# Sliding-window attention and a gated feed-forward: the first k and q loads split by head and by token

## The chip, the cores and the metric

The kernel runs on one core of one Trainium2 chip. TensorE (PE in the profile) multiplies matrices, VectorE (DVE), ScalarE (ACT) and GpSimd (POOL) work on SBUF, and SyncE (SP) only issues transfers here. Loads that POOL issues go through one software queue and may change the type on the way (float32 in DRAM to float16 in SBUF); loads and stores that SP issues go through a hardware queue and keep the type. All of them run on the core's 16 DMA engines. The metric is the device time of one execution in microseconds; three runs of the kernel before gave 304.77, 305.67 and 306.55, median 305.67.

## The reference

For 8 batches, 8 heads, 576 tokens and 64 numbers per head, each token attends to itself and the 63 tokens before it; the result, laid out as 4608 tokens by 512, goes through a gated feed-forward.

```python
scores = scale * np.matmul(q, k.transpose(0, 1, 3, 2))
mask = (rel >= 0) & (rel < 64)          # rel = row - column
attn = softmax(np.where(mask, scores, -1e9))
x = (attn @ v).transpose(0, 2, 1, 3).reshape(4608, 512)
gate = np.maximum(x @ w_gate, 0.0)      # 512 x 1536
out = (gate * (x @ w_val)) @ w_out      # 1536 x 512
```

## The kernel before

**Tiling.** The feed-forward runs over nine tiles of 512 tokens. Attention goes by windows of 64 queries against 128 keys. Heads are handled in two halves of four (`hh` 0 and 1), each head on 32 partitions. A load of k or q puts 32 partitions x 1152 numbers per head into `nat`; a DVE transpose of 32 x 32 blocks (`qk_trans`, L254) turns that into `kT` or `qT`, from which TensorE makes scores (`score_run`, L276). ACT takes the exponential, TensorE multiplies by v (`value_block`), DVE divides by the sum (`norm`) and turns the result into `xt` (`turn`, L306), the input of the feed-forward.

**First part (L313).** The start is written out by hand. SP loads k and q of the first four heads of batch 0 as float32 into the room of `vs`, which is not needed yet (L318); DVE and ACT each round one half of every row to float16 (`rounded`, L339). POOL loads k and q of the other four heads (L320), three parts of v, and the four parts of the first column block of w_gate and w_val (L332 to L334). DVE turns k and q of heads 0 to 3, then of heads 4 to 7. Then come scores and exponentials for tokens 0 to 383, values, and the turned `xt`. POOL copies part of v (L378) before it issues anything more.

**Second part (L418).** All later work is a list of named operations (`op`), each with the operations that it comes after. `ORDER` (L24) is a list, written into the kernel, of these operations in the order in which they are issued: each entry has the number of the operation, a letter for its engine (P, A, D, G, S) and the buffers that it takes. A key in microseconds that each `op` carries, and the numbers in `K`, do not reach the chip: an engine simply works through its own entries in the order of the list and waits in each for what it needs. An operation behind a waiting one on the same engine waits too. A PSUM bank passes on when the operation that gives it back is done.

The weights come in column blocks 0, 1 and 2 of 512, each in two halves by input row. Tile 0 uses them plainly: groups of matmuls for gate and value (`direct_halves` L679 for block 0, `direct_block` L636 for blocks 1 and 2), a relu on ACT, a product on DVE, and then w_out in three blocks (L858). Later tiles use a scheme with seven products in place of eight (L784, L948), which needs sums and differences of the weights (`us`, `vs`, L733; `ts`, L892).

The matmul groups of tile 0 are named by their numbers in the changed list (numbers from 11 up are smaller by 6 in the list before): 42 to 63 are block 0, 82, 86, 90 and 94 the gate groups of block 2, 66, 70, 74 and 78 the gate groups of block 1, 98, 102 and 106 (gate) and 99, 103 and 107 (value) the last 128 tokens, 22 the scores of the last three windows of batch 0 in tile 0, 173 and 178 the scores of tile 1, 149 the first group of w_out.

```python
            run = op("scores", key, pe(0.0081 * 8 * n + 0.0268 * n), lambda e: score_run([st[g] for g in range(G)], items),
                     after=after, take=[("bank", st, range(G))])
            exps.append(op("exp", key + kt("e") + 0.6 * g, act(64 * n), exp, after=[run], take=[("p", pp, (g,))], give=[("bank", st, g)]))
```

Of the kernel before, what the change touches and what calls it, by code (L numbers as in the profile page):

```python
# [10 lines left out]
FP32 = mybir.dt.float32  # L11
# [10 lines left out]


ORDER = """  # L24
29S 3G 30S 2G 42P0 36P4 31S 37P5 0G 43P6 1G 32S 33S 38P 11G 44P 34S 48P1 46Ai 54P2 12G 35S 40Aj 56P 39P 58Ak 6G 49P3
51P 7G 55P7 57P 150G 45P 59D 50P 47D 52Al 76P7 4G 41D 80P0 112D 78Am 53D 84P4 148G 114D 16P2615 116D 72P3 20Ag 156G
120D 17Ah 64P5 19A8 5G 82An 60P7 14D 18A9 13D 118D 21P2 24P1 68P0 122G 25D 22D 26D 88P6 70Ao 28D 164G 23D 74Ap 85P1
27D 62Aq 157G 77P0 104D 66Ar 113D 96P7 86As 152G 124D 90At 79D 115G 81P2 98Ak 87D 89P3 83D 8G 93P5 151D 110G 92P4 149D
117G 94Ai 95D 167P6012 160G 121D 73P4 171Aa 119D 154G 123D 65P7 168Ab 9G 106D 61P5 159A 111D 10G 15D 158A 69P2 75D
163G 97P6 91D 169Ac 325G 67D 100P4 170Ad 71D 105G 153D 102Aj 327G 143P3 125D 329G 128P7 99D 161A 107G 162A 177P0 101P1  # L30
178D 108G 155D 180P2 138P4 126G 181D 63D 182D 109G 144P 179D 103D 139P 331G 192D 172P6520 482D 133P1 174Ae 483D 486D
176Af 134P 165D 173A8 485G 145P 175A9 326D 166A 135P 490G 140P 136Al 328D 146Am 183P5 186P0 141As 334G 147S 184D
344P6213 137S 185D 142S 337G 187D 202P4 193D 348Ag 200P5 341G 196D 347Ah 189P3 129P 188D 346Aa 333G 487D 201An 130P
190D 340G 191D 203Ai 195D 215P1 523G 345Ab 214P0 197D 131Ap 224P2 194D 198G 210P 132S 225At 332D 226P3 211Ar 204P6
127G 239P 227Ao 205D 216P 240Ak 212P 199D 217Aq 241P 330D 491G 339S 207P6 213Aj 335S 228P 206A 336S 218D 220P 493G
249P 338S 221Am 208D 233P 343S 242Al 222D 243P6 209G 230P 229As 234D 251P 250Ap 527G 244D 236P 252Ai 354P5 525G 237D
259P 231An 261P 355D 219A 356D 232G 349P0614 245A 357P5 524D 223G 260An 305P7 351Ac 253P2 358D 262As 529G 359D 256P6
352Ad 266P3 263G 254D 246P5 353A8 257D 264P1 255A 709G 268P 489D 271P 265Am 247D 258G 281P4 267Aq 269D 278P5 350A9
274P 248G 282D 276P 275An 279D 360P2 363P0 277As 366P4 532G 369D 284P 235A 286P 364D 531G 361D 310P5 285Ai 362D 270A
367D 238G 377P2 370D 287Ap 306P 365D 280A 373G 294P 371D 378Ao 288P0 368D 296P 283G 289D 311P 297At 372D 295Aj 291P4  # L40
535G 374D 379P3 272D 381P1 375G 380Ar 387P 382D 299P 388Am 389P 298G 300D 391P6 390Aq 393P 292D 301A 384P1 376G 528D
397P 394Aj 307P 536S 398At 273G 395D 342S 312P 290A 385D 537S 383A 302P 534S 410P 308Ak 386G 303D 407P 533S 405P 526D
408Al 392P0 539G 313Ao 315P7 399D 304G 396A 542P1435 411D 406Ar 316P 713G 530D 545Ae 409G 544Af 320P6 546Aa 413P 715G
543Ab 547P2345 538G 414D 412A 321P 710D 549Ag 415G 548Ah 552P1 555P0 550A8 401P3 553D 711G 554D 420P2 551A9 293G 556D
403P4 557D 402An 558P1 561P5 404As 421D 564P0 416P 718G 562D 422A 418P 563D 423P2 400G 417Al 559D 560D 317P 419Ar 568D
433P5 717G 318Am 424D 428P 426P 721G 319S 565D 429Aq 309S 566D 430P1 314S 570D 427Ai 441P2 425G 541S 438P 567D 442Ap
443P0 439Aj 436P 431D 571G 451P 444At 569D 322P 437An 434D 455P4 452As 440G 453P 432A 456D 575P3 454Am 448P 572D 445P
484G 323Aj 449D 463P 576An 324S 465P4 446D 540S 464Ak 435G 461P 712D 720S 458P6 462Ao 577P5 722S 573G 457A 473P 466D
719S 471P 578Ai 468P1 723S 459D 474Aq 585P 469D 460G 476P 586Aj 582P6 477D 467A 479P 725G 587P 492D 472Ap 498P7 583D
447A 475G 579P0 480D 478A 499P 580D 588At 450G 728P4261 716D 500Ap 591P 729Ac 574G 595P 714D 592Aq 589P0 501P4 732Ad  # L50
488G 593D 596Al 502P 730Aa 590P1 481G 503D 603P 731Ab 608P 597D 504S 581A 605P 470G 609D 738P2 606Ar 741P4 601P6 739D
740D 604Am 584G 611P 742D 602As 733P0523 743D 594A 612D 724G 616P 736Ae 494D 599P4 895G 735Af 628P1 899G 621P2 495D
600Ak 618P5 737A8 614P 607G 619D 505P 615Ao 622D 506P 734A9 897G 496D 624P 617Ai 727S 744P3 625An 747P5 598G 750P2
626P 748D 507Ap 749D 631P0 610A 745D 634P 746D 907G 511P 627Am 629D 904G 639P5 497D 630A 508P3 903G 620A 509P 751D
752D 640Ar 623G 636P 632D 643P 635Al 649P 510Aq 644D 613G 646P 650Ak 641P2 754D 515P 642As 633G 647D 656P4 637Aj 753D
# [105 lines left out]
def kernel(  # L161
# [85 lines left out]
    def heads_of(b, name, hh):  # L247
        src = (q if name == "q" else k)[b, G * hh:G * hh + G]
        return src.rearrange("h (i j) d -> (h i) (j d)", i=32)

    def qk_load(b, name, hh):
        nc.gpsimd.dma_start(nat[name, hh], heads_of(b, name, hh))

# [59 lines left out]
    def first_part():  # L313
# [3 lines left out]
        for name in "kq":  # L317
            nc.sync.dma_start(t32[name], heads_of(0, name, 0))  # L318
# [745 lines left out]
```

## Time and profile before

| what | value |
|---|---|
| median of three runs | 305.67 us (304.77 to 306.55) |
| the profiled execution | 306.52 us |
| its span | 304.80 us |
| PE busy | 292.8 us, 96% of the span |
| DVE, POOL, ACT busy | 243.8, 237.5, 213.5 us |
| granted TensorE clock | 0.999 |
| DRAM read, written | 37.75 MB, 9.44 MB |

Loads of the first part by the trace: k and q of heads 0 to 3 issued by SP at 0.82 and 1.26 us, landed at 5.45 and 6.83; k and q of heads 4 to 7 issued by POOL at 1.31 and 2.05, landed at 8.25 and 10.18; three parts of v landed at 11.00, 11.56 and 12.25; block 0 of the weights landed at 13.54, 14.80, 16.04 and 17.87.

| POOL's next loads, in order | issued | landed |
|---|---|---|
| w_gate block 2, second half | 13.61 | 20.00 |
| w_gate block 2, first half | 14.30 | 21.26 |
| w_gate block 1, first half | 15.00 | 22.54 |
| w_gate block 1, second half | 15.69 | 23.79 |
| v of batch 0, 128 rows; 64 rows | 16.39; 17.26 | 24.68; 25.12 |
| w_val block 2, first; second half | 17.93; 18.62 | 26.36; 27.64 |
| q of batch 1, heads 0 to 3 | 20.55 | 29.09 |
| w_val block 1, first half | 21.54 | 30.36 |
| k of batch 1, heads 0 to 3 | 22.82 | 31.75 |
| v of batch 1, 128 rows | 24.08 | 32.92 |
| w_val block 1, second half | 24.97 | 35.15 |
| v of batch 1, 64 rows; 128 rows | 26.83; 27.55 | 35.59; 36.41 |
| k of batch 1, heads 4 to 7 | 28.42 | 37.85 |
| w_out block 0 | 30.52 | 40.37 |
| v of batch 1, 128 rows | 33.53 | 41.21 |
| q of batch 1, heads 4 to 7 | 34.44 | 42.60 |
| w_out blocks 1; 2 | 34.98; 35.71 | 45.21; 47.71 |

How to read the profile: the span is cut into stretches with the busy time of each engine in it; a timeline line has the start, the duration, the engine, the line of the kernel, the operation with output and input, how many were merged, and in brackets the idle time of the engine before it and what ended it. A wait for several things is put under the name of the one that came last by the profile. The load of a transfer is seen from its issue to its landing. DMA records give each packet's start, duration and size.

### The profile page before, as it was taken

Reading aid. Unit: us, or ns where it says so; the run is one execution under the profiler, and the core shown is the slowest. Engines: PE = TensorE matmul, PEld = TensorE weight load, DVE = VectorE, ACT = ScalarE, POOL = GpSimd, SP = SyncE. Lnnn points to the kernel's source line nnn. Section 1 sums busy time; section 2 is a strip of 40 time slices with the busy share of each in tenths; the row PEclk is TensorE's granted clock in tenths of the full one; section 3 lists DMA queues with packets and bytes.
Section 4 is the critical chain, followed back from the end, with each engine's and each line's share of the span. In section 5 each row is a group of like instructions: output and inputs, shape, how many; then the busy total and the mean of one; then the engine's idle time right before and its main releaser. Section 6 shows DMA issues by size and latency. Waiting matters only on the chain.

```text
span 304.8 us, 11222 instructions
## 1 busy us (share of the span) xinstructions
PE 292.8 (96%) x4793; PEld 242.3 (79%) x4793; DVE 243.8 (80%) x424; ACT 213.5 (70%) x417; POOL 237.5 (78%) x235
## 2 busy tenths in 40 slices
PE   7789889999999999999999999999999999999993
PEld 4566655778767888888888888888888888888883
DVE  5966977998878898888888898989788588677772
ACT  4545535888687888778668878777778678778720
POOL 8678986699999799798687798989898376777610
PEclk9999999999999999999999999999999999999999
DMA  7999999988559932962969549261940301100224
GB/s 215 185 184 200 192 202 157 199 179 113 39 86 131 185 72 44 165 61 80 151 69 183 94 65 154 28 163 9 99 107 3 105 5 34 37 1 2 71 94 147
DMA packets 59586, 32.87 MB, mean 108 GB/s; under 512 B 39440, under 2 KB 54416, under 8 KB 59536
## 3 DMA queue, kind: packets, MB, share of 16 engines
q0 software_dynamic: 46672, 18.29, 51.8%
q1 hardware_dynamic: 12720, 13.80, 14.6%
q8 instruction: 37, 0.61, 0.8%
q14 instruction: 13, 0.11, 0.1%
q10 hardware_dynamic: 144, 0.07, 0.1%
HBM read 37.75 MB, written 9.44 MB: 155 GB/s over the span
## 4 chain that ended last, share of the span: by engine, by line
PE 86%; DMA 8%; POOL 2%; DVE 2%; issue 1%; ACT 0%; DVEq 0%; POOLq 0%; ACTq 0%
PE bank L784 49%; PE bank L948 21%; PE bank L858 7%; PE bank L296 4%; DMA wo<-in_moe_w_out_dram 3%; PE bank L290 3%; DMA wg<-in_moe_w_gate_dram 2%; DMA v<-in_v_dram 2%; PE bank L282 2%; PE bank L649 1%; POOL v L261 1%; DVE xw L303 0%; POOL v L378 0%; DVE qT L258 0%; POOL vs L733 0%
## 5 line engine op out<-in xcount | busy, mean ns | idle before, releaser
L818 POOL TENSOR_TENSOR g_sb<-pr,pr 128x512 f16<-128x512 f32 x96 | 121.2, 1277 | 25.5 <-ACT pr L831 6.8
L800 DVE TENSOR_TENSOR pr<-bank,pr 128x512 f32<-128x512 f32 x144 | 94.5, 683 | 28.4 <-PE bank L784 19.1
L793 ACT COPY pr<-bank 128x512 f32<-128x512 f32 x144 | 81.1, 590 | 26.3 <-PE bank L784 21.7
L784 PE MATMUL bank<-xt,vs 128*128 128x256 f16 x384 | 55.7, 273 | 0.0
L784 PE MATMUL bank<-xt,us 128*128 128x256 f16 x384 | 54.9, 273 | 0.0
L809 ACT ACTIVATE pr<-pr 128x512 f32<-128x512 f32 x72 | 45.1, 638 | 2.2 <-DVE pr L800 1.9
L544 ACT ACTIVATE p<-bank 128x512 f16<-128x512 f32 (+1 forms) x68 | 36.7, 594 | 13.8 <-PE bank L290 13.5
L784 PE MATMUL bank<-xt,wg 128*128 128x256 f16 x288 | 42.8, 273 | 0.0
L784 PE MATMUL bank<-xt,wv 128*128 128x256 f16 x288 | 41.8, 273 | 0.0
L784 PEld LDWEIGHTS <-vs 128*128 128x128 f16 x384 | 36.9, 98 | 5.6
L784 PEld LDWEIGHTS <-us 128*128 128x128 f16 x384 | 37.1, 98 | 4.7
L261 POOL DMA_DIRECT2D v<-in_v_dram x40 | 34.9, 878 | 4.0 <-PE bank L296 3.3
L831 ACT ACTIVATE pr<-bank 128x512 f32<-128x512 f32 x48 | 28.1, 604 | 12.2 <-PE bank L784 11.4
L948 PEld LDWEIGHTS <-g_sb 128*128 128x128 f16 x336 | 32.8, 98 | 3.8
L948 PE MATMUL bank<-wo,g_sb 128*128 128x256 f16 x252 | 32.4, 273 | 0.0
L784 PEld LDWEIGHTS <-wg 128*128 128x128 f16 x288 | 27.9, 98 | 4.0
L784 PEld LDWEIGHTS <-wv 128*128 128x128 f16 x288 | 27.9, 98 | 3.3
L948 PEld LDWEIGHTS <-ss 128*128 128x128 f16 x252 | 24.4, 98 | 2.9
L303 DVE TENSOR_TENSOR xw<-bank,r 128x448 f16<-128x448 f32 (+2 forms) x45 | 25.2, 568 | 1.0
L308 DVE STREAM_TRANSPOSE xt<-xw 128x512 f16<-128x512 f16 (+2 forms) x38 | 25.2, 671 | 0.4
L858 PE MATMUL bank<-wo,g_sb 128*128 128x512 f16 x96 | 23.2, 380 | 1.3 <-DMA wo<-in_moe_w_out_dram 1.0
L615 POOL TENSOR_TENSOR xt<-xt 128x512 f16<-128x512 f16 x15 | 17.3, 1156 | 6.5 <-DVE xt L615 4.4
(105 smaller groups left out, 388.5 us busy)
## 6 DMA issues: line engine op xcount, KB each, us to landing
out_dram<-pr SPq DMA_DIRECT2D x35, 256.0 KB, 2.6
k<-in_k_dram POOLq DMA_DIRECT2D x15, 288.0 KB, 6.0
q<-in_q_dram POOLq DMA_DIRECT2D x15, 288.0 KB, 6.5
v<-in_v_dram POOLq DMA_DIRECT2D x32, 128.0 KB, 5.3
v<-v SPq DMA_DIRECT2D x24, 66.0 KB, 2.1
v<-v SPq DMA_DIRECT2D x12, 132.0 KB, 3.0
wg<-in_moe_w_gate_dram POOLq DMA_DIRECT2D x6, 256.0 KB, 7.2
wv<-in_moe_w_val_dram POOLq DMA_DIRECT2D x6, 256.0 KB, 8.9
```

The source lines that it names most:

```text
L261: nc.gpsimd.dma_start(v16s[b % 2][lo:hi, g, :, 0:64], v[b, :, 64 * g - 64 + lo:64 * g - 64 + hi].rearrange("h p d -> p h d"))
L303: nc.vector.tensor_tensor(x, blocks_of(to, n)[:, :, 0:D].rearrange("p s (c e) -> p s e c", e=2), r[:, :, :, None].to_broadcast([128, n, 2, ...
L308: nc.vector.transpose(xt[:, 2 * hh:2 * hh + 2, c0:c0 + n].rearrange("p e (s c) -> p s e c", c=32), x)
L544: nc.scalar.activation(pp[g][:, 0:n].rearrange("p n c -> p (n c)"), st[g][:, 0:64 * n], ACT.Exp, scale=scale)
L784: nc.tensor.matmul(slot[to][:, HT * m:HT * m + HT], w[:, kk, 128 * m:128 * m + 128], x[:, kk], start=(first and m == 0 and kk == 0), stop= ...
L793: lambda e, hold=hold, slot=slot: nc.scalar.copy(hold["x"], slot["A"]),
L800: nc.vector.tensor_tensor(hold["x"], slot[to], hold["x"], ADD)
L809: lambda e: nc.scalar.activation(hold["x"], hold["x"], ACT.Relu), after=[o])
L818: lambda e: VEC[e].tensor_tensor(gh[:, fs:fs + 2, h], pair(a["x"]), pair(b["x"]), MUL),
L831: lambda e, hold=hold, slot=slot, i=i: nc.scalar.activation(hold["x"], slot["A"], ACT.Copy if i else ACT.Relu),
L858: nc.tensor.matmul(bank["b"][:, 0:c1 - c0], gs[t % 2][:, f, 128 * sub:128 * sub + 128], wo[:, f, c0:c1], start=(j == 0 and i == 0), stop=( ...
L948: nc.tensor.matmul(bank[to][:, HD * m:HD * m + HD], a[:, f, 128 * m:128 * m + 128], b[:, f], start=(first and m == 0 and f == 0), stop=(f ...
```

## The change

Only tokens 0 to 383 are scored in the first part, so k and q of tokens 384 to 575 of heads 0 to 3 are not needed there. The changed kernel loads heads 0 to 3 of batch 0 in two steps, and each step in one transfer per head (32 partitions): first 384 tokens of k and of q (eight transfers of 32 x 3072 bytes), later the other 192 tokens (eight of 32 x 1536 bytes) into the room of the second `g_sb` buffer. Both go over SP. The second part is rounded to float16 by ACT or DVE and turned by DVE as operations of the list (`rest_load`, `round`, `rest_turn`: numbers 11 to 16). The scores of the last three windows of batch 0 (22, and 173 for tile 1) now come after these, and the load of batch 1 into the same room after the rest is turned. `QSPLIT` is 0, so its branches are not taken; `FIRST` is not used.

```diff
-        n = S // 32 * D
+        U2 = 2 * U
+        n = U2 // 32 * D
         for name in "kq":
-            nc.sync.dma_start(t32[name], heads_of(0, name, 0))
-        for name in "kq":
-            qk_load(0, name, 1)
+            by_head(nc.sync, t32[name], 0, name, 0, 0, U2)
+        qk_load(0, "k", 1)
...
+            qk_load(0, "q", 1)
...
+    def by_head(queue, to, b, name, hh, lo, n):
+        src = (q if name == "q" else k)[b, G * hh:G * hh + G, lo:lo + n]
+        for g in range(G):
+            queue.dma_start(to[32 * g:32 * g + 32], src[g].rearrange("(i j) d -> i (j d)", i=32))
...
-        qk_trans(0, "k", 0)
+        qk_trans(0, "k", 0, 0, U2)
         rounded("q", nc.scalar.copy, nc.vector.tensor_copy)
-        qk_trans(0, "q", 0)
+        qk_trans(0, "q", 0, 0, U2)
...
+        def load_rest():
+            lo, n = 2 * U, S - 2 * U
+            for i, (name, hh) in enumerate([("k", 0), ("q", 0)] + [("q", 1)] * QSPLIT):
+                to = gs[1].rearrange("p f n -> p (f n)").bitcast(FP32)[:, n // 32 * D * i:n // 32 * D * (i + 1)]
+                load = op("rest_load", kt("l00") + 0.1 * i, {"SP": (1.4, False)}, lambda e, to=to, name=name, hh=hh: by_head(nc.sync, to, 0, name, hh, lo, n),
+                          dma=(0.2, "store", "sp"))
+                rounded = op("round", kt("l00") + 3.0 + 0.1 * i, {"ACT": (0.49, False), "DVE": (0.35, False)},
+                             lambda e, to=to, name=name, hh=hh: (nc.scalar.copy if e == "ACT" else nc.vector.tensor_copy)(nat_of(name, hh, lo, n), to), after=[load])
+                loads[0, name, hh] = rounded
+                turns[0, name, hh] = op("rest_turn", kt("l01") + 0.1 * i, {"DVE": (0.46, False)}, lambda e, name=name, hh=hh: qk_trans(0, name, hh, lo, n),
+                                        after=[rounded])
...
-            after = [turns[b, nm, hh] for b in batches if b for hh in halves for nm in "kq"]
+            after = [turns[b, nm, hh] for b in batches for hh in halves for nm in "kq" if (b, nm, hh) in turns]
```

`ORDER` is another list from its first entries to its last: no engine keeps its old order for more than a few entries, 24 operations sit on another engine, and the number of operations grows by the six new ones. Where the two lists differ at the start, in the numbers of the changed kernel:

| queue | before | changed |
|---|---|---|
| POOL's loads after the first part | as in the table above | w_gate block 2 (second, first half), block 1 first half, v 64 rows, v of batch 1 128 rows, v 128 rows, w_gate block 1 second half, w_val block 2 (first, second half), block 1 second half, q of batch 1, w_val block 1 first half, k of batch 1, v of batch 1 128 rows, q and k of batch 1's heads 4 to 7, v of batch 1 128 rows, w_out 0, 1, 2, v of batch 1 64 and 128 rows |
| TensorE, block 0 | 48 42 43 49 44 50 54 60 62 45 55 57 61 63 51 56 | 48 42 49 43 54 55 60 51 62 50 44 56 57 45 61 63 |
| TensorE, then | 82 86 90, scores 22, 78 70 66 | 82 94 86 90, scores 22, 78 70 66 |
| TensorE, before w_out | ... 173 79 71 67 75 103 106 149 | ... 79 71 173 106 103 107 75 149 |
| TensorE, behind 149 | 134 183 107 186 144 150 | 134 67 183 186 144 150 |
| DVE, first entries | products 65 53 47, weight difference 118, product 59, weight differences 120 122 126 | weight difference 124, products 53 65, rest turn 16, product 47, round 12, rest turn 13, product 59, weight difference 110 |
| ACT, first entries | relu 52 46 64 58 84 | relu 52 58 46 64, round 15, relu 88 92 |

## The prediction

> **What bounds the kernel now.** I read the stretches first, then who TensorE waits for, then its timeline, then the DMA queues. The stretches (PE busy is the second number):
>
> ```profile
> 21.30:40.40 19.10, 17.36 (x288) 12.04 (x288) 16.33 (x37) 10.16 (x21) 16.30 (x20) 1.00 1.47 195
> 40.40:46.00 5.60, 5.27 (x88) 2.93 (x89) 3.42 (x8) 1.26 (x2) 5.08 (x6) 1.00 1.40 202
> 46.00:76.00 30.00, 30.00 (x604) 21.99 (x602) 26.14 (x49) 23.71 (x45) 24.32 (x26) 1.00 1.04 162
> ...
> 286.00:300.00 14.00, 14.00 (x129) 12.33 (x126) 9.40 (x18) 4.74 (x9) 3.82 (x3) 1.00 0.29 95
> ```
>
> From 46 us to its end at 300 us TensorE never pauses and its clock is fully granted. So after 46 us nothing can be gained, only lost, and the change is decided by how late TensorE is when it enters that stretch. Its waits after 14 us:
>
> ```profile
> PE bank L858 <- DMA wo<-in_moe_w_out_dram: 1.0, 1, 1.0
> PE bank L649 <- DMA wg<-in_moe_w_gate_dram: 0.9, 1, 0.9
> PE bank L649 <- DMA wv<-in_moe_w_val_dram: 0.7, 1, 0.7
> ```
>
> and where they stand:
>
> ```profile
> 21.30 2.12 PE L649 MATMUL bank<-xt,wg 128*128 128x384 f16 x12 [0.91 <-DMA wg<-in_moe_w_gate_dram]
> ...
> 35.19 3.34 PE L649 MATMUL bank<-xt,wv 128*128 128x384 f16 x30 [0.70 <-DMA wv<-in_moe_w_val_dram]
> 38.37 1.06 PE L649 MATMUL bank<-xt,wg 128*128 128x128 f16 x16
> 40.42 1.90 PE L858 MATMUL bank<-wo,g_sb 128*128 128x512 f16 x8 [0.99 <-DMA wo<-in_moe_w_out_dram]
> ...
> 45.26 1.02 PE L858 MATMUL bank<-wo,g_sb 128*128 128x512 f16 x4 [0.31 <-DVE xw L303]
> ```
>
> Each is a wait for weights; the 0.31 stands under a DVE name, but block 1 of w_out landed at 45.21. The loads of POOL's queue land one behind another without a gap until 54 us, 1.26 us per 256 KB weight part, 1.42 per k or q, about 0.83 per 128-row v, 0.44 per 64-row v, 2.5 per block of w_out (successive landings). So a transfer's place in that queue is its landing time. The queues on the page:
>
> ```profile
> q0 software_dynamic: 46672, 18.29, 51.8%
> q1 hardware_dynamic: 12720, 13.80, 14.6%
> q8 instruction: 37, 0.61, 0.8%
> ```
>
> The instruction queue matters: its 16 KB packets each hold one DMA engine for 0.9 to 1.1 us (DMA records at 15.8 and 32.4 us), and right behind these two the landings step by 1.8 and 2.1 us (wg, wv: 17.87, 20.00) and by 2.2 us (wv at 35.15) where 1.26 is normal.
>
> **The change, part by part.** The sum is made against the profiled execution (306.52 us, span 304.80, 1.72 around it); the median shown is 305.67, 0.85 lower, and the difference is put on the median.
>
> *First loads.* Two issues of 0.39 and 0.42 us on SP become eight; at 0.42 the last q piece is issued at 0.82 + 7 x 0.42 = 3.8 instead of 1.26. Eight more for the rest stand directly behind them. Their key says 15 us, but nothing on SP holds them except that each waits for the landing of a first piece, so they go at about 4 to 7 us, ahead of v and the weights: no byte leaves the front of the stream. SP's next work is a store at 52.68; nobody is held behind. When does q land (6.83 before)? From below, as a free 66 KB move: 3.8 + 2.1 = 5.9. From above, as the stores at 52.68 to 57.52 that met POOL's loads:
>
> ```profile
> out_dram<-pr SPq DMA_DIRECT2D x35, 256.0 KB, 2.6
> ...
> v<-v SPq DMA_DIRECT2D x24, 66.0 KB, 2.1
> ...
> out_dram<-pr SPq DMA_DIRECT2D x4, 256.0 KB, 5.5
> ```
>
> (the last row is of 52 to 58 us, the first two of the whole run): 3.8 + 5.5 = 9.3. Before, both loads were queued before the first POOL load got a packet (5.09 us); now k of the other four heads, issued at 1.31, can come between, since lone POOL loads show their first packet 1.3 us after issue. The loaded row is nearer: I take 8.
>
> *Rounding and turning for 384 tokens.* By two thirds of their rows the DVE cast of k goes from 0.69 to 0.46 us, each turn from 1.26 to 0.84. That does not pull the front in: q of the other four heads landed at 10.18 and its turn started at 10.20; the v parts landed at 11.0, 11.56 and 12.25. With q at 8: + 0.47 + 0.84 = 9.3, two full turns to 11.8, against 11.46: the first gate matmul (14.44) 0.35 late. Ends: 0 with q at 5.9, 1.6 with q at 9.3.
>
> *Block 0 of gate and value.* 64 matmuls, 5.5 us. The new order puts three groups that need tokens 192 to 383 ahead of those that need the second halves of the weights; those tokens were turned at 16.70, so TensorE stands about 0.8 us there and ends near 20.95 instead of 20.39. This and the late front stay under the wait that ends at 21.30 (0.35 us is left of it), then under the two waits below (0.2 and 0.9 us): a front up to 1.4 us late costs nothing; its upper end would cost 0.2.
>
> *DVE at 21 us.* Its queue now has a weight difference (waits for wg, 21.26; 0.42) ahead of four products of block 0 (0.49 each), the two rest turns (0.42 each) and one rest cast (0.35). These ran at 19.84 to 22.2 before; now they end about 24.9. Waiting for them: a PSUM bank (matmul group 94, 0.3 us late) and scores 22, which now also need the rest turns and the relu behind group 90: start about 25.05 against 23.36 before. TensorE pauses 0.6 us, and then group 78 waits for the second half of wg block 1. That was landing 4 behind 20.00 (23.79); now three v parts stand ahead of it: 22.54 + 0.44 + 0.85 + 0.85 + 1.26 = 25.95, a pause of 0.2 more. From there the steps of the timeline (0.70 for a 384-column group, 1.06 for a 128-column one of block width, scores 0.95) bring TensorE to the first w_out group at about 41.3; nothing between waits more than 0.3 us (scores 173 on the turn of k, landed near 34).
>
> *The w_out load, where it is decided.* Ahead of block 0 of w_out POOL's queue now also has q of batch 1's second half and a 128-row v part, and no longer a 64-row v part: 1.42 + 0.83 - 0.44 = 1.8 us. It landed at 40.37; now 42.2. POOL issues it near 31 (30.52 before), far ahead of the stream, so the order and not the issue counts.
>
> *Are 32-row pieces dearer?* DMA records: 178 ns for 4608 bytes, 96 for 2048, 47 for 1056. Between them 3072 bytes take about 125 and 1536 about 70. Per engine 16 x 178 = 2.85 us become 16 x (125 + 70) = 3.1, and 14 more completion writes of 9 ns add 0.13: +0.4. Ends: -0.3 (POOL's loads fill gaps of SP's) and +0.8 (1536 bytes as dear as 2048, half the gaps unused). I take +0.3: w_out at 42.5.
>
> *Sum.* TensorE starts w_out at 42.5 instead of 40.42: +2.08. Ahead of it is now a 128-column group (107, 1.06) and no longer a 384-column one (67, 0.70): -0.36. Block 1 of w_out follows 2.5 behind block 0 instead of 4.84 (v and q no longer stand between), so the 0.31 at 45.26 goes. +2.08 - 0.36 - 0.31 = +1.4: span 306.2, profiled 307.9, on the median **307.1 us**. What is late next: nothing until the end, if the new order keeps TensorE fed after 46 us as the old one did.
>
> One rule speaks against the pieces more strongly. The 64-row moves of this trace (1056 bytes in 47 ns, 22.5 bytes per ns) show nearly the pace of 128-row loads (25.9), so I price rows by length alone. The Trainium skill, SBUF — State Buffer, "Door 1: The DMA port swizzle", says that a transfer to 32 partitions reaches 8 of 16 ports and gives 189 GB/s against 328 for 128 partitions; by that rule 1.18 MB would take, as an estimate, some 2.6 us longer, and the sum would be near +3.7. The trace's row disagrees so far, on 64 partitions and not on 32.
>
> **Rivals.**
> - *Half-speed pieces, slower.* If a 32-row piece holds its engines twice as long, 2 x 3.1 - 2.85 = 3.3 us at worst and, with POOL's loads filling half, 1.6 at least reach w_out: +2.7 to +4.4, 308.4 to 310.1. It decides from 0.5 us on. This is the case that the page on SBUF describes. For it: pieces of one head lie in one quarter of the partitions. Against: the 47 ns.
> - *New pauses after 46 us, slower.* Every queue's order is new to the end. DVE at 26.14 of 30 us and POOL at 27.25 leave little room; ten pauses like the 0.2 to 0.3 us ones listed for the front, or one late product per tile, give +2 to +4 on top of part of the 1.4: 308 to 311. Against: the old order has no pause there.
> - *w_out on time, not slower.* The slow landing at 35.15 holds 0.95 us that came from an instruction packet hitting the engine already last; of four such packets from 8 to 33 us two did that. If it misses, w_out lands at 41.5, TensorE's own arrival (41.3) nearly decides, and the sum is 41.5 - 40.42 - 0.67 = +0.4: 306.1; with POOL's loads filling SP's gaps, +0.2.
> - *Faster.* If the rest really stood behind the first weights, 393 KB at 25.9 x 16 bytes per ns, 0.95 us, would leave the front, and the 0.91 at 21.30 would go. It would show only if w_out came early too, and its bytes ahead are fixed. At most -1.7: 304.0. The eight rest issues would have to wait, and nothing in the queue makes them.
>
> **How the numbers follow.** Chances: the forecast's case 0.55 (its own range 306.1 to 308.1: one instruction packet less or more is 0.95 either way); half-speed 0.08; new pauses 0.15; w_out on time 0.18; faster 0.04. 0.5% (1.5 us) is about what a measurement of this kernel tells from no change: 304.1 to 307.2 on the median. The forecast's case lies across the upper edge, 0.30 inside and 0.25 above. Faster 0.04, same 0.30 + 0.18 = 0.48, slower 0.25 + 0.08 + 0.15 = 0.48. The range 305.4 to 309.3 leaves out the faster case and the upper half of the two slow ones.
>
> **What would show it.** Right: no wait of TensorE after 46 us; one near 25.5 to 26 for wg; the w_out wait ending near 42.5 and being the last; the SP rest issues at 4 to 7 us; first gate matmul between 14.4 and 16. Wrong: rest issues near 15 us; w_out landing before 41; w_out matmuls starting without a DMA wait; pauses after 46 us; 3072-byte packets far over 125 ns.

## The result and the profile after

The changed kernel takes **308.88 us** (median of six runs, 307.43 to 309.81) against 305.18 for the kernel before (six runs beside it): the ratio is 1.0115, with a 95% interval of 1.009 to 1.014. It is slower by about 3.5 us, where 1.4 was forecast. 308.88 lies inside the range that was given (305.4 to 309.3), but above the forecast's own case (306.1 to 308.1): it is in the part that had been added for two slower rivals.

The traces show less than the medians: the profiled execution after took 308.51 us (span 306.8), that of before 306.52. The trace of before is one of its slower executions (1.3 above the median of the six; later medians of the same kernel are 304.95 to 305.59), that of after one of its faster ones (0.4 below). Of the 3.7 between the medians the pair of traces can explain 2.0; how much of a median a pause in one trace accounts for is therefore read below from medians of edited kernels.

TensorE's timeline of the changed kernel (start, duration, engine, line, operation, number merged, idle time before it and what ended it) answers to the one shown of before. First the start of the one before:

```profile
9.24 0.55 PE L290 MATMUL bank<-qT,kT 32*128 32x64 f16 x48 [1.21 <-DVE qT L258]
10.02 1.56 PE L358 MATMUL bank<-zero 128*128 128x384 f32 x4 [0.23 <-ACT p L370]
...
14.44 0.82 PE L696 MATMUL bank<-xt,wg 128*128 128x192 f16 x8 [0.23 <-DVE xt L308]
```

After:

```profile
11.85 0.55 PE L299 MATMUL bank<-qT,kT 32*128 32x64 f16 x48 [2.73 <-DVE qT L267]
12.64 2.93 PE L374 MATMUL bank<-zero 128*128 128x384 f32 x4 [0.24 <-ACT p L386]
15.50 0.67 PE L299 MATMUL bank<-qT,kT 32*128 32x64 f16 x48
...
18.36 0.82 PE L725 MATMUL bank<-xt,wg 128*128 128x192 f16 x8
...
20.71 0.49 PE L725 MATMUL bank<-xt,wg 128*128 128x192 f16 x4 [0.88 <-DVE xt L317]
...
24.67 2.76 PE L678 MATMUL bank<-xt,wg 128*128 128x384 f16 x16
...
28.01 0.27 PE L291 MATMUL bank<-ident,biasT 32*128 32x128 f16 x5 [0.41 <-ACT pr L688]
...
42.88 1.90 PE L887 MATMUL bank<-wo,g_sb 128*128 128x512 f16 x8 [0.34 <-DVE g_sb L690]
```

The first gate matmul (18.36) starts 3.92 us later than before (14.44), the first block-2 group 3.37 later (24.67 against 21.30), the first w_out group 2.46 later (42.88 against 40.42), and the last matmul ends 2.35 later (302.39 against 300.04). All three weight waits of before are gone: what was waiting is now lateness of TensorE itself, and it begins at 9 us, with a pause of 2.73 for q. The 0.34 at 42.88 has DVE's name, but w_out block 0 landed at 42.83, 0.05 before it; in the kernel before the same step was 0.05 (40.37 and 40.42).

Two lines of DVE's timeline show what the pause waits for, and the table of DMA issues up to 16 us (transfers, KB each, median us from issue to landing) how long a piece took:

```profile
10.43 0.36 DVE L357 CAST q<-vs 128x384 f16<-128x384 f32 x1 [2.52 <-DMA vs<-in_q_dram]
10.96 0.85 DVE L267 STREAM_TRANSPOSE qT<-q 128x384 f32<-128x384 f32 x1 [0.16 <-ACT q L357]
```

```profile
vs<-in_k_dram SPq DMA_DIRECT2D x4, 96.0 KB, 2.9
vs<-in_q_dram SPq DMA_DIRECT2D x4, 96.0 KB, 5.5
...
k<-in_k_dram POOLq DMA_DIRECT2D x1, 288.0 KB, 4.7
q<-in_q_dram POOLq DMA_DIRECT2D x1, 288.0 KB, 6.1
```

Before, the same table had:

```profile
vs<-in_k_dram SPq DMA_DIRECT2D x1, 576.0 KB, 4.6
vs<-in_q_dram SPq DMA_DIRECT2D x1, 576.0 KB, 5.6
```

The last pieces of k and q landed at 6.22 and 10.31 (5.45 and 6.83 before), though they carry a third less; POOL's k and q of heads 4 to 7, which nobody needed yet, landed at 6.04 and 8.14 (8.25 and 10.18). The stretches of the first microseconds (last two numbers: DMA share and GB/s) show it as a flow. Before:

```profile
2.00:3.00 1.00, 1.00 (x44) 1.00 (x41) 0.93 (x4) 0.30 (x2) 0.93 (x5) 1.00 0.76 221
3.00:4.00 1.00, 0.51 (x20) 0.41 (x16) 0.00 (x0) 0.00 (x0) 0.86 (x4) 1.00 0.87 323
4.00:5.00 1.00, 0.61 (x9) 0.27 (x10) 0.18 (x1) 0.00 (x0) 1.00 (x3) 1.00 1.03 424
5.00:6.00 1.00, 1.00 (x5) 0.47 (x4) 0.53 (x1) 0.53 (x1) 1.00 (x2) 1.00 1.11 293
6.00:7.00 1.00, 1.00 (x5) 0.49 (x4) 0.89 (x2) 0.63 (x4) 1.00 (x2) 1.00 1.07 196
```

After:

```profile
2.00:3.00 1.00, 1.00 (x44) 1.00 (x41) 0.93 (x4) 0.31 (x2) 0.93 (x5) 1.00 0.85 177
3.00:4.00 1.00, 0.51 (x19) 0.41 (x16) 0.00 (x0) 0.00 (x0) 0.86 (x4) 1.00 0.61 95
4.00:5.00 1.00, 0.59 (x9) 0.27 (x10) 0.18 (x1) 0.00 (x0) 1.00 (x2) 1.00 1.14 248
```

The three microseconds from 2 to 5 moved 968 KB before and 520 after. Not all of that is lost flow: the records of POOL's loads have the size as written, in float16 (288 KB in the table for 576 KB of float32): 2304 bytes in 192 ns, 12 bytes per ns, where SP's whole loads have 4608 in 178, 25.9. So a stretch full of POOL's packets shows no more than some 196 GB/s (before, 6 to 7 us, share 1.07). The DMA records add whose packets they were: before, POOL's first packet started at 5.09 us, when most of SP's were through; after, it started at 2.77, and in each microsecond from 3 to 7 SP's packets held only 0.16 to 0.26 of the DMA engines' time. POOL's first packets were slow besides: the first twelve took 306 to 909 ns, where the first twelve before took 191 or 192.

The stretches further on (the number before the DMA share is the granted clock):

```profile
14.00:21.30 7.30, 6.12 (x172) 4.23 (x171) 5.84 (x15) 3.37 (x15) 7.24 (x11) 0.87 1.20 196
...
46.00:76.00 30.00, 29.77 (x597) 21.48 (x598) 25.96 (x47) 21.99 (x42) 24.20 (x26) 1.00 1.11 172
```

Behind the pause for q the granted clock fell: 0.87 is the mean of a stretch, and within it the clock was 0.50 from 12.5 to 15.8 us and 1.00 from 15.9 on. Four filler matmuls (products with zeros that nothing reads) took 2.93 us where they took 1.56 before. After 46 us only small pauses (0.23 at 58.6) are new in this execution.

### The profile page after: what moved, and what is told of

The parts are those of the page before. It is cut to its first block, busy times and chain, and to the rows that moved or that the text cites. A ratio compares the mean times of both kernels' runs of the same rounds, so it can differ in the third digit from the quotient of the medians.

```text
span 306.8 us, 11261 instructions
## 1 busy us (share of the span) xinstructions
PE 294.7 (96%) x4793; PEld 243.1 (79%) x4793; DVE 242.5 (79%) x423; ACT 212.9 (69%) x419; POOL 240.4 (78%) x238
## 4 chain that ended last, share of the span: by engine, by line
PE 84%; DMA 7%; POOL 4%; issue 2%; DVE 1%; ACT 0%; POOLq 0%; DVEq 0%; ACTq 0%
PE bank L813 48%; PE bank L977 21%; PE bank L887 7%; PE bank L305 3%; DMA k<-in_k_dram 3%; DMA v<-in_v_dram 3%; PE bank L299 2%; DMA wg<-in_moe_w_gate_dram 2%; PE bank L291 2%; POOL v L270 1%; POOL us L762 1%; POOL q L260 1%; DVE g_sb L690 0%; POOL k L260 0%; POOL v L394 0%
## 5 line engine op out<-in xcount | busy, mean ns | idle before, releaser
L813 PE MATMUL bank<-xt,vs 128*128 128x256 f16 x384 | 56.7, 273 | 0.4 <-issue 0.2
L813 PE MATMUL bank<-xt,us 128*128 128x256 f16 x384 | 55.7, 273 | 0.1
L572 ACT ACTIVATE p<-bank 128x512 f16<-128x512 f32 (+1 forms) x68 | 35.8, 592 | 13.1 <-PE bank L299 13.0
L813 PE MATMUL bank<-xt,wv 128*128 128x256 f16 x288 | 42.8, 273 | 0.0
L813 PE MATMUL bank<-xt,wg 128*128 128x256 f16 x288 | 42.1, 273 | 0.0
L977 PE MATMUL bank<-ts,ss 128*128 128x256 f16 x168 | 21.6, 273 | 0.0
```

The lines of the kernel that those rows point to most:

```text
L572: nc.scalar.activation(pp[g][:, 0:n].rearrange("p n c -> p (n c)"), st[g][:, 0:64 * n], ACT.Exp, scale=scale)
L813: nc.tensor.matmul(slot[to][:, HT * m:HT * m + HT], w[:, kk, 128 * m:128 * m + 128], x[:, kk], start=(first and m == 0 and kk == 0), stop= ...
L977: nc.tensor.matmul(bank[to][:, HD * m:HD * m + HD], a[:, f, 128 * m:128 * m + 128], b[:, f], start=(first and m == 0 and f == 0), stop=(f ...
```

## The experiments

Each was timed against the kernel before on its chip, with the ratio beside it; the time of a kernel alone moves by some tenths with the chip (the kernel before: 304.95 to 305.59).

**Whole first loads.** The new order stays; the pieces and the rest go.

```diff
-        n = U2 // 32 * D
+        n = S // 32 * D
...
-            by_head(nc.sync, t32[name], 0, name, 0, 0, U2)
+            nc.sync.dma_start(t32[name], heads_of(0, name, 0))
...
-    ... lambda e, to=to, name=name, hh=hh: by_head(nc.sync, to, 0, name, hh, lo, n),
+    ... lambda e: None,
...
-    ... lambda e, to=to, name=name, hh=hh: (nc.scalar.copy if e == "ACT" else nc.vector.tensor_copy)(nat_of(name, hh, lo, n), to), after=[load])
+    ... lambda e: None, after=[load])
```

> The changed kernel, but k and q of the first four heads come whole again (576 tokens, one transfer each, rounded whole in the first part); the loads and the rounding of the rest are gone, the turns of the rest and the whole new order of every queue stay. Front theory (the pieces made q land at 10.3 us, the first gate matmul started 3.9 us late, and that lateness is the loss): q lands near 6.9, first gate matmul near 14.6, and the time falls by 2 us or more, to 306 to 307. Queue theory (w_out block 0 stands too far back in POOL's order, 42.8 us): the front comes back all the same, but TensorE then waits for w_out, which lands at 42.2 to 42.6; the time falls by at most 0.6, to 308.2 or more. Two-limits theory (TensorE's own arrival at 42.5 and w_out's landing at 42.8 stand side by side, so that lifting one alone gives little): as the queue theory here; it differs from it in the next kernels.

306.69 us, ratio 1.0041 (1.0013 to 1.0069). Its timeline of TensorE:

```profile
14.95 0.82 PE L725 MATMUL bank<-xt,wg 128*128 128x192 f16 x8 [0.26 <-DVE xt L317]
...
40.08 1.90 PE L887 MATMUL bank<-wo,g_sb 128*128 128x512 f16 x8 [0.90 <-DVE g_sb L690]
...
65.70 0.28 PE L305 MATMUL bank<-v,p 128*32 128x65 f16 x12 [1.15 <-DMA v<-v]
```

q landed at 6.65, the front is back, and 2.2 us of the median with it, as the front theory said. Not expected by any theory: w_out block 0 landed at 40.03 and not at 42.2 to 42.6. The pieces and the rest had pushed the whole stream back, not only q: the first weight part landed at 13.37 here, at 15.11 in the changed kernel, at 13.54 before. And there is a new wait of 1.15 us at 65.7, to which I come below.

**w_out block 0 earlier in POOL's order**, ahead of the v part (166) and the q load (160):

```diff
-... 128D 166G 66P7 130D 72Ao 116D 27P6 160G ... 97D 8G 83P5 ...
+... 128D 66P7 130D 72Ao 116D 27P6 ... 97D 8G 166G 160G 83P5 ...
```

> The changed kernel with one edit in the written order: on POOL's queue the load of w_out block 0 goes ahead of the 128-row v part and of q of batch 1's second half, as before the change. Its landing should move up by 0.83 + 1.42 = 2.2 us, from 42.8 to 40.6. Queue theory: the first w_out matmul starts 1.5 to 2 us earlier and the time falls to about 307. Front theory and two-limits theory: TensorE itself does not get there before 42.5, so the wait of 0.34 goes and no more: 308.3 to 308.9.

309.35 us, ratio 1.0102 (1.0070 to 1.0135): no change. w_out landed at 40.30, and TensorE came to it, without a wait, at 43.24:

```profile
19.23 0.82 PE L725 MATMUL bank<-xt,wg 128*128 128x192 f16 x8
...
43.24 1.89 PE L887 MATMUL bank<-wo,g_sb 128*128 128x512 f16 x8
```

So in the changed kernel the place of w_out does not decide: TensorE itself comes later than the load. The queue theory, which my forecast stood on, falls here.

**Both edits.**

> Both edits together: whole first loads, and w_out block 0 ahead of the v part and the q load. Two-limits theory: only here does the time fall, by about 2 us or more, to 306 to 306.9, with w_out landing near 40.3 and the first w_out matmul at 40.5 to 41.5. Front theory: as with whole loads alone. Queue theory: as with w_out earlier alone. If the new order of the other engines costs something after 46 us, the time stays above 307 though the first w_out matmul is early.

305.34 us, ratio 0.9996 (0.9975 to 1.0017): with whole loads and w_out as early as before, the new order of everything else costs nothing that can be measured.

```profile
14.51 0.82 PE L725 MATMUL bank<-xt,wg 128*128 128x192 f16 x8 [0.23 <-DVE xt L317]
...
39.50 1.89 PE L887 MATMUL bank<-wo,g_sb 128*128 128x512 f16 x8
```

The four kernels as ratios to before:

| | w_out as changed | w_out earlier |
|---|---|---|
| pieces and rest | 1.0115 | 1.0102 |
| whole loads | 1.0041 | 0.9996 |

The pieces and the rest cost 0.7 to 1.1% (2.3 to 3.2 us), whichever way w_out stands. The place of w_out costs 0.45% (1.4 us) with whole loads, where the two intervals just touch, and nothing that can be measured with pieces: the late front hides it. The two-limits theory is right in that part, but wrong in that one edit alone already brought 2.2 us.

**The pieces alone, in the kernel before** (all 576 tokens, four transfers per tensor, no rest, the old order):

```diff
-            nc.sync.dma_start(t32[name], heads_of(0, name, 0))
+            for g in range(G):
+                nc.sync.dma_start(t32[name][32 * g:32 * g + 32], (q if name == "q" else k)[0, g].rearrange("(i j) d -> i (j d)", i=32))
```

> The kernel before the change with one edit: each of the two first loads of SyncE is made in four pieces of one head (32 partitions, 4608 bytes each, all 576 tokens) instead of one transfer; no rest, no new order. q should land late again, 8 to 10.5 us, for eight issues of 0.42 us and POOL's loads between. Front theory: the time rises by 2 us or more, to 307.2 or more. Two-limits theory: the waits of TensorE for weights (0.91, 0.70, 0.99) take up some 2.6 us of a lateness of 3 to 4, so the time rises by 0.3 to 1.3, to 305.5 to 306.5. Queue theory: no more than 0.3. If 32-partition pieces hold the DMA engines longer, w_out lands 1.6 us or more later than 40.4 as well and the time rises by 1.6 or more.

309.95 us, ratio 1.0137 (1.0104 to 1.0170): 4.2 us above before by the ratio, as only the front theory and the clause on dearer pieces allowed.

```profile
20.77 0.83 PE L697 MATMUL bank<-xt,wg 128*128 128x192 f16 x8
...
43.67 1.89 PE L859 MATMUL bank<-wo,g_sb 128*128 128x512 f16 x8
```

The split by head does the damage by itself: q landed at 11.85, the first gate matmul came 6.3 us late, and the waits of 0.91, 0.70 and 0.99 were used up long before w_out. The stream was late as well (first weight part 14.79 against 13.54, w_out 42.19 against 40.37), but TensorE did not come to w_out before 43.67. The other half of the change, 384 tokens in place of 576, helps against this (q at 10.31 in the changed kernel), without making up for it.

**POOL's first loads a little later.**

```diff
+        if not QSPLIT:
+            bands()
         qk_load(0, "k", 1)
...
-        if not QSPLIT:
-            bands()
```

> The changed kernel with one move: GpSimd builds its two masks before it issues the loads of k and q of heads 4 to 7 (now after). Those two issues go from 1.32 and 2.06 us to about 2.7 and 3.4, so their first packets from 2.77 to about 4. If q of the first heads is late because POOL's packets come between the pieces, q lands at 7.5 to 9 instead of 10.3, the first gate matmul starts 1 to 2.5 us earlier than 18.4, and the time falls by 0.7 to 2 us, to 307 to 308.2. If the pieces of 32 rows are slow in themselves, q lands at 9.8 or later and the time does not fall (308.5 to 309.5); it would rise if the two POOL loads, which then land later, come to be what the front waits for.

310.23 us, ratio 1.0170 (1.0136 to 1.0204). A miss: q landed at 10.83, later than in the changed kernel. Its DMA issues say why:

```profile
vs<-in_k_dram SPq DMA_DIRECT2D x4, 96.0 KB, 2.2
vs<-in_q_dram SPq DMA_DIRECT2D x4, 96.0 KB, 6.0
```

POOL's issues (2.27 and 3.01 us) now fell behind the last piece of k and behind the first of q, and its first packet came at 3.72. The pieces of k took 2.2 us (median); those of q, with POOL's packets, 6.0. So pieces of 32 rows are not slow by nature to the extent seen in q.

**q on ScalarE's queue, and then w_out earlier besides.**

```diff
-            by_head(nc.sync, t32[name], 0, name, 0, 0, U2)
+            by_head(nc.scalar if name == "q" else nc.sync, t32[name], 0, name, 0, 0, U2)
```

> The changed kernel, but the four first pieces of q are issued on ScalarE's queue and no longer on SyncE's behind those of k, so that all eight pieces are issued by about 2.2 to 2.6 us (now 4.4). If what makes q late is that its pieces are issued one after another by one engine while POOL's packets start at 2.77, q lands at 6.5 to 8.3 and k a little later than its 6.2; the first gate matmul starts 2 us or more earlier, and the time falls to 306.5 to 307.7. If the shares of the DMA engines decide and not the issue, q still lands at 9 or later and the time stays above 308.

> As the last, with w_out block 0 ahead of the v part and the q load on POOL's queue besides. If the front comes back, this should be worth 1.3 us more, as it was with whole loads (306.69 to 305.34): 305.2 to 306.4. If the front does not come back, it is worth nothing, as in the changed kernel (308.9 to 309.3).

308.08 us (1.0104, 1.0069 to 1.0139) and 308.36 us (1.0095, 1.0061 to 1.0128), neither as low as hoped; the first is above 308, as the expectation has it where the shares of the DMA engines decide. With two engines issuing, k and q share the lateness: in the first k landed at 8.56 (6.22 in the changed kernel), with q behind by little (its cast started at 9.91 without a wait); in the second they landed at 8.46 and 8.63. The first gate matmul came at 17.14, 1.2 earlier, and the first w_out group in the second at 40.96, 1.9 earlier. All of that was lost again in two pauses later on, in the second:

```profile
57.30 0.60 PE L813 MATMUL bank<-xt,vs 128*128 128x256 f16 x4 [0.87 <-issue]
67.79 0.28 PE L305 MATMUL bank<-v,p 128*32 128x65 f16 x12 [1.36 <-DMA v<-v]
```

**More filler in the pause.** Does the lower clock cost time?

```diff
-        keep_hot(st[1][3][:, 0:2 * U])
+        for _ in range(4):
+            keep_hot(st[1][3][:, 0:2 * U])
```

> The changed kernel with three more of the filler matmuls (0.74 us each, multiplied by zeros, nothing reads them) in the stretch in which TensorE waits for q (9.1 to 11.85 us). No data comes earlier. If the loss of clock behind that pause is part of the loss (the four fillers after it took 2.93 us instead of 1.56, the granted clock 0.94 and 0.87), the second run of scores starts 1 to 1.4 us earlier, so does the first gate matmul, and the time falls by 0.5 to 1.4 us, to 307.5 to 308.4. If not, it stays at 308.9.

309.15 us, ratio 1.0136 (1.0102 to 1.0170): no gain, although the front does come earlier. The fillers behind the first scores took 1.56 again and the first gate matmul came 1.1 earlier; the first w_out group was at 41.45, 1.4 earlier; then:

```profile
13.04 1.56 PE L374 MATMUL bank<-zero 128*128 128x384 f32 x4 [0.23 <-ACT p L387]
...
17.26 0.82 PE L726 MATMUL bank<-xt,wg 128*128 128x192 f16 x8
...
56.96 0.61 PE L814 MATMUL bank<-xt,wv 128*128 128x256 f16 x4 [0.46 <-ACT p L573]
67.77 0.28 PE L305 MATMUL bank<-v,p 128*32 128x65 f16 x12 [1.23 <-DMA v<-v]
```

So the lost clock is worth 1.1 us at the front, and pauses further on, the larger near 66 us, took it back. That one is for the moves of v on chip over SP's queue. In this trace the second of them was issued at 61.37 and landed at 67.72, 0.2 behind the q load that POOL issued at 61.86 (67.49). In the changed kernel the first two moves landed in good time (67.04; TensorE came at 67.41).

**All pieces ahead of POOL.** POOL's loads go behind its masks and three sets of constants:

```diff
+        if not QSPLIT:
+            bands()
+        nc.gpsimd.memset(zero32, 0.0)
+        for i in range(2):
+            v_fixed(i, nc.gpsimd)
         qk_load(0, "k", 1)
...
-        for i in range(2):
-            v_fixed(i, nc.vector)
-        nc.vector.memset(zero32, 0.0)
-        if not QSPLIT:
-            bands()
```

> The changed kernel with GpSimd's two loads of heads 4 to 7 held back behind its masks and three sets of constants (which VectorE wrote until now), so that they are issued near 4.5 us and their packets start near 5.8, after the last piece of q has been issued. The four pieces of k of the last kernel but three landed 2.1 to 2.5 us after their issue while no GpSimd packet ran. If GpSimd's packets are what holds the pieces up, all pieces of q now land by 6.5 to 7.3, the wait for q goes, heads 4 to 7 land at 8.5 and 10.7, and the first gate matmul starts at 14.8 to 16; the time falls to 306.7 to 308. If pieces of 32 rows are slow whatever runs beside them, q lands at 9 or later and the time stays at 308.9 or above.

(The kernel that this text counts back to is the one with POOL's first loads a little later.) 308.78 us, ratio 1.0117 (1.0088 to 1.0146): the time does not move. POOL's issues went to 3.70 and 4.44 and not to 4.5. The first piece of q landed at 4.76, 2.1 us after its issue; the other three, in whose time POOL's packets began (5.16), landed at 6.68, 6.92 and 8.71, so that the edit spared one piece and not all. The first gate matmul came at 17.01, 1.35 earlier, but POOL's whole stream had moved back with its first loads (first weight part at 16.08):

```profile
10.25 0.83 PE L299 MATMUL bank<-qT,kT 32*128 32x64 f16 x48 [2.46 <-DVE qT L267]
...
17.01 0.82 PE L725 MATMUL bank<-xt,wg 128*128 128x192 f16 x8
...
42.76 1.90 PE L887 MATMUL bank<-wo,g_sb 128*128 128x512 f16 x8 [0.97 <-DMA wo<-in_moe_w_out_dram]
```

Now TensorE waits 0.97 us for w_out: the front theory's gain met the queue theory's bound, the other side of the table above. The same kernel shows how the pieces flow with nothing beside them (3 to 5 us), and what happens when POOL's packets begin (5 to 6):

```profile
3.00:4.00 1.00, 1.00 (x28) 0.68 (x26) 0.00 (x0) 0.00 (x0) 0.94 (x4) 1.00 0.71 200
4.00:5.00 1.00, 1.00 (x4) 0.45 (x3) 0.36 (x1) 0.49 (x2) 1.00 (x2) 1.00 0.79 219
5.00:6.00 1.00, 1.00 (x5) 0.47 (x4) 0.85 (x1) 0.35 (x3) 1.00 (x3) 1.00 0.87 100
```

200 to 219 GB/s at a DMA share of 0.71 to 0.79, where whole loads reached 323 and 424; and about 100 in the microsecond in which POOL's packets set in. In the kernel before the microsecond of that start moved 293 GB/s, SP's packets among them.

What held the pieces at 200 to 219? SP hands over a piece of 98,304 bytes every 0.46 us, which is 214 GB/s by itself. Two kernels shown above bear on it, from 2 to 3 us: the kernel before with pieces (147,456 bytes each, the same pace of issue), and the first with q on ScalarE's queue (two engines issuing):

```profile
2.00:3.00 1.00, 1.00 (x44) 1.00 (x41) 0.93 (x4) 0.30 (x2) 0.93 (x5) 1.00 0.95 254
2.00:3.00 1.00, 1.00 (x44) 1.00 (x42) 0.93 (x4) 0.31 (x1) 0.93 (x5) 1.00 0.93 283
```

With more bytes per issue, or with a second engine that issues, the pieces flow faster, at a DMA share of 0.93 to 0.95. So it was the pace of issue that held one queue of 96 KB pieces. What would hold them above 283 is not shown, since POOL's packets begin at 2.81 and 3.08 us in these two.

**The q load of the third batch held back**, first with whole loads, then with w_out earlier too. It tests the bound near 66 us.

```diff
-... 348S 531G 257P ... 236P 215G 240D ...
+... 348S 257P ... 236P 215G 531G 240D ...
```

> Whole first loads as before, and in the written order of GpSimd the load of q for the third batch, issued at 60.5 us, goes behind the next product (to about 63.5). With whole loads TensorE waits 1.15 us at 65.7 for the moves of v on SyncE's queue, of which the second took 5.9 us from issue to landing beside that load. If the load holds the moves up, the pause goes and the time falls by 0.6 to 1.1, to 305.6 to 306.1 (that is most of what w_out earlier gave with whole loads, 1.35). If the moves are late for another reason, or another wait takes over, the time stays at 306.4 to 307.

> The three edits together: whole first loads, w_out block 0 earlier, and the q load of the third batch held. If the pause at the moves of v is there in many executions of the kernel with the first two edits (its profiled execution, 304.73, had none; its median is 305.34), the median falls by 0.3 to 0.7, to 304.6 to 305.0. If not, it stays at 305.3.

305.89 us (1.0017, 0.9989 to 1.0046) and 304.85 us (0.9991, 0.9970 to 1.0012). In the first the moves of v landed at 64.1 to 66.0, the q load now being issued at 64.94, and the pause at 65.7 is gone from the trace. Against the kernels without this edit the ratios fall by 0.0024 and 0.0005, in the expected direction; the intervals overlap, so the size is not shown. It also means that part of what the table puts down to the place of w_out may be this pause, which the trace of whole loads has and that of both edits has not. The second is the best kernel of the study, and its interval does not tell it from the kernel before.

**w_out earlier in the kernel before.** Was that wait the bound there?

```diff
-... 86As 152G 124D ... 83D 8G 93P5 ...
+... 86As 8G 152G 124D ... 83D 93P5 ...
```

> The kernel before the change with one edit in the written order of GpSimd: the load of w_out block 0 goes ahead of the load of k of batch 1's second half (1.44 us), so it should land near 38.9 instead of 40.37. In the kernel before, TensorE waits 0.99 us for it at 40.42 and then never again to the end. If that wait sets the end, the time falls by 0.7 to 1.0, to about 0.997 of before (304.3 to 304.7). If the moves of v near 65 us are the next bound right behind it, or a load that now lands 2.5 us later is waited for, the time stays within 0.3 of before.

305.42 us, ratio 1.0005 (0.9987 to 1.0022). No gain: w_out block 0 landed at 38.00 and was not waited for, and block 1, at 44.18, was:

```profile
38.45 1.89 PE L858 MATMUL bank<-wo,g_sb 128*128 128x512 f16 x8
...
44.23 1.89 PE L858 MATMUL bank<-wo,g_sb 128*128 128x512 f16 x8 [1.26 <-DMA wo<-in_moe_w_out_dram]
```

Taking one load forward handed the wait to the next; that the stream as a whole is the bound there would explain it, but is not shown. In its trace the last matmul ended 1.07 earlier than in that of before (298.97), and the medians agree: a difference of 1 us between two single traces is not evidence here.

## Why the prediction was right or wrong

- *Direction and size.* Slower, by 3.5 us and not 1.4. The forecast's case, a late w_out load as the one cause, is not what happened. That 308.88 lies inside the range is luck as far as that case goes: the range reached up there for rivals that had 0.23 together, and the cause was neither of them as I had put it, but a late front.
- *When q lands: the step that failed.* I took 8, with 5.9 and 9.3 as ends; it was 10.31. The upper end came from 256 KB stores met by POOL's loads (5.5 us). The last piece of q took 5.9 from its issue at 4.39, but I had put that issue at 3.8, and I had used the upper row as a bound, though nothing made it one. I had written that POOL's k "can come between" and did not follow it to the end: POOL's packets did not share the engines evenly, they held four fifths of them. The cleanest sign is one piece, the first of q, issued at 2.65 us in three kernels: it landed at 4.76 where POOL's first packet came at 5.16, at 7.94 where it came at 3.72, and at 8.24 (the changed kernel) where it came at 2.77. The Trainium skill, DMA: Bandwidth & Descriptors, "Queues, rings and completion order", says that each engine goes round the queues that have work and drains a whole packet of some 9 to 17 descriptors before it switches. If an engine switched after each transfer, a piece of 32 rows (two records per engine of 134 ns) against a POOL load of 128 rows (eight of 192) would give SP, as an estimate, 0.27 / (0.27 + 1.54) = 0.15 of an engine's time, near the 0.16 to 0.26 of the trace. That condition is mine, and the trace of before does not fit it: POOL's first packet there came at 5.09, when 228 of the 256 packets of SP's two loads had started, and not behind the first load's 128, although the same issue (1.31 us) had its first packet at 2.77 in the changed kernel. No run here changed the number of rows alone, so why POOL's share is so large stays open.
- *The front.* "A front up to 1.4 us late costs nothing" was not tested as such; the front was 3.9 late. The first scores started 2.6 late (11.85 against 9.24), for q. The other 1.3 came behind them, most of it from the clock (1.1 by the filler experiment), which I had left out altogether: four fillers behind the pause took 2.93 in place of 1.56. With whole loads and the new order it was 0.5 late (14.95), and the wait for w_out, 0.90 long, took that up.
- *The wait at 20.7.* I forecast about 0.8 us for tokens 192 to 383, and 0.88 is there, as are 0.87 to 0.88 in the edited kernels with the new order.
- *The waits from 21 to 42 us.* The pause of 0.6 at scores 22 came as one of 0.41, at 28.01 and not near 25. The 0.2 for w_gate at 25.95 did not come: TensorE was late enough (28.45 for group 78, with the load landed at 26.30). The issues of the rest, put at 4 to 7 us, went out at 4.86 to 10.33: the last four waited each for a piece of q.
- *w_out at 42.5: right by two errors.* It landed at 42.83. By their own steps (1.42 and 0.85, less 0.44) the two extra loads are worth the 1.8 that I gave them. But the pieces cost the stream 1.6 us at the first weight part (15.11 against 13.54), not 0.3, and the slow steps of the stream, which I left as they were, gave back some 0.8: 1.83, 2.13 and 2.23 before (2.4 over the normal 1.26) against one of 2.84 after (31.55 to 34.39, 1.6 over). I had put them down to instruction packets. That does not hold for the one after: its packets (20.19, 26.20 and 35.33 us) stand elsewhere, and no slow step follows the first two. What makes such a step is open. With whole loads the same two loads stand ahead of w_out, and it landed at 40.03, no later than before: from trace to trace the slow steps differ by as much as the whole term.
- *The price of pieces.* Packets of 3072 and 1536 bytes took 148 and 90 ns in the mean (medians 134 and 78), where I had 125 and 70; whole packets of 4608 took 214 in the mean, where I had used their 178. Per engine that is 16 x (148 + 90) = 3.8 us against 3.4: the difference of 0.4 is the one I had, both terms being too small. The 47 ns for 1056 bytes, on which I priced rows by length alone, was the value of undisturbed packets; the median of all of them is 67. Where the rest of the 1.6 us went is not settled: POOL's first packets took 306 to 909 ns in place of 191, and the share of 0.61 from 3 to 4 us counts packets by their start, so that it leaves out what such long packets held of that microsecond (0.83 with it, 0.93 before).
- *Rival "half-speed pieces".* I gave it 0.08. The Trainium skill, SBUF — State Buffer, "Door 1: The DMA port swizzle", has 32 partitions reach 8 of the 16 ports. In time it was nearer than my case (2.3 to 3.2 us for the pieces, by the table). Its mechanism is not borne out. For it seemed 200 to 219 GB/s for pieces alone against 323 and 424, but the pace of issue accounts for that. Against it: the fastest quarter of the 3072-byte packets took 121 ns, 25.4 bytes per ns, as fast as whole loads (25.9); the engines were not full; and pieces flowed at 254 and 283 GB/s when more bytes were issued per us. Pieces of several heads were in flight together there, so this is not a measurement of one transfer to 32 partitions.
- *Rival "new pauses after 46 us".* Not in the trace of after (0.23 at 58.6), but real: whole loads, q on ScalarE and more filler each show 0.6 to 1.4 us at the moves of v. It becomes visible as soon as the front is earlier.
- *Rival "w_out on time", 0.18.* It took TensorE's own arrival to be 41.3, from a front that was on time. It was 42.5 (42.88 less 0.34).
- *The reading "from 46 us on it can only lose"* holds for the trace of before. What it suggests, that a wait taken away ahead of 46 us is a gain, does not: with w_out earlier, the median of the kernel before did not move.

What stays open: why POOL's packets take so large a share of the engines, and why its first packets are slow; what the eight transfers of the rest cost apart from the first eight; and what 384 tokens in one transfer for k and one for q would have cost, since no run has the split by token without the split by head. That the medians lie 1.7 us further apart than the two traces is within the scatter of single executions (304.77 to 306.55 before, 307.43 to 309.81 after).

## What to carry to other kernels

In this kernel a transfer cut into pieces lost more than the time of its packets: its place among the other queues' packets was lost too, because the later pieces met what another queue had started meanwhile. Ask of each piece what else is in flight when it is issued, and take the landing of the last piece as the price. When a load is off the path by a microsecond, the next load, or the next queue, is often a microsecond behind it: test both together before one is called the cause.

## What the runs showed that I had not expected

- Where POOL's first loads began among pieces, they started badly: in the changed kernel their first twelve packets took 306 to 909 ns, and the microsecond behind their start (3 to 4) moved 95 GB/s (83 and 100 in the two kernels with POOL's loads later), against 196 when POOL's packets fill the engines. Where they began behind whole loads of SP, the first packets took 191 ns.
- The same piece of 96 KB, issued at the same time on the same queue, took 2.1 us or 5.3 to 5.6 us, by when POOL's packets began.
- A 66 KB move on SP's queue took 6.4 us when a POOL load was issued 0.5 us behind it (61.37 to 67.72), 3.8 when that load came later (60.66 to 64.45).
- Filler matmuls in a pause of TensorE brought the granted clock from 0.87 to 1.00 in the stretch behind it (14 to 21.3 us), and no time.
